# Attention times values, turned round: exponentials stationary, values and a column of ones moving, and a DMA transpose after it

## The chip, the cores and the metric

The kernel runs on one core of a Trainium2 chip. The metric is the device time of one execution in microseconds, the median of several; the profiled execution has a span of its own, about 2 us shorter. TensorE (PE in the profile) multiplies, VectorE (DVE) and ScalarE (ACT) work elementwise, GpSimd (POOL) helps, SyncE (SP) issues the DMAs.

## The reference, cut to what matters

Cosine attention over 8 batches, 12 heads, 448 positions and 64 channels, then a feed-forward part with 3584 tokens:

```python
scores = np.matmul(q_n, k_n.transpose(0, 1, 3, 2)) / tau      # q_n, k_n: rows scaled to length 1
attn = np.exp(scores - max); attn = attn / sum(attn)
x = (attn @ v)  ->  (3584, 768)
h = x @ w_in;  g = h * sigmoid(1.702 * h);  out = g @ w_out   # 768 -> 2048 -> 768
```

The kernel keeps the scores with keys on partitions and works on pairs of heads: 48 pairs, six to a batch.

## The kernel before

A planner written in Python walks all operations with estimated durations before the kernel is built and fixes the order on each engine. The first two batches (pairs 0 to 11) go through a half-width path with exponentials stationary, 112 columns at a time. The other 36 pairs have values stationary, one attention block for each head:

```python
def attend(x, j):                      # pair x, head j of the pair
    ps = ps_a.tile([128, S], FP32, tag="a")            # one bank, a single buffer
    for c in range(C):                                 # 4 chunks of 112 keys
        nc.tensor.matmul(out=ps,
            lhsT=vts[x % NV][:, c, j],                 # 112 x 128: 64 values, a one, zeros
            rhs=exps[x, c][:, j],                      # 112 x 448 exponentials move
            start=(c == 0), stop=(c == C - 1))
def attended(x, j):                    # VectorE: PSUM to SBUF, scaled, denominators as a row
    ...
# for each group of three pairs: two DMAs of the denominators to DRAM, one back as 112 x 24,
# a reciprocal on VectorE, one DMA out, two that spread it over 64 partitions each
def normalise(x):                      # VectorE: two multiplications SBUF x SBUF
    ...
```

The result stands with channels on partitions, as the feed-forward product wants it, but the denominators are one row that has to reach 64 partitions; hence the trip through DRAM.

## Time and profile before

| | before |
|---|---|
| median time | 471.35 us (3 runs), 470.99 with the run made beside the changed kernel |
| span of the profile | 467.7 us |
| busy TensorE / ScalarE / VectorE | 454.7 / 302.3 / 273.6 us |
| attention block, full width | 0.76 us, 72 of them |
| first score matmul of the full-width part | at 100.7 us |
| last attention block ends | at 402.9 us |

The lines behind it stand in the prediction. Idle time and distances given below without a line are taken from the starts and ends in the traces.

### The profile page before, as it was taken

The numbers are of one execution on the slowest core, as the hardware profiler recorded it, in microseconds if no ns is written. First come the engines' busy times: TensorE is split into PE (matmuls) and PEld (weight loads), VectorE is DVE, ScalarE is ACT, GpSimd is POOL, SyncE is SP. The second block draws the span as 40 slices with busy tenths as digits, with TensorE's granted clock in tenths as the row PEclk, the third lists the DMA queues.
The fourth block names the chain that finished last, engine by engine and source line by source line (L and its number), as shares of the span: only waits on it lengthen the run. The fifth ranks groups of instructions, "written<-read, shape, count | busy, mean of one in ns | idle before, by whom it ended". The sixth has DMA issues, their size and how long they took to land.

```text
span 467.7 us, 8829 instructions
## 1 busy us (share of the span) xinstructions
PE 454.7 (97%) x3306; PEld 259.6 (56%) x3306; DVE 273.6 (59%) x651; ACT 302.3 (65%) x478; POOL 146.7 (31%) x209
## 2 busy tenths in 40 slices
PE   8899999999999998999999999999999999999996
PEld 8778988644445544455445554455445554565563
DVE  6857986767899538682785539771463216523500
ACT  5878577879998567866886668755666457414421
POOL 2837573377354525133341505124010000000000
PEclk9999999999999999999999999999999999999999
DMA  8999098999976687455634747434301212021022
GB/s 234 245 241 244 4 196 185 265 253 310 251 163 160 142 189 167 119 142 150 170 96 111 214 126 166 132 97 103 84 2 31 69 35 64 1 78 54 1 68 69
DMA packets 81434, 63.49 MB, mean 136 GB/s; under 512 B 40232, under 2 KB 74864, under 8 KB 81392
## 3 DMA queue, kind: packets, MB, share of 16 engines
q1 hardware_dynamic: 77504, 56.41, 48.3%
q0 software_dynamic: 3648, 6.29, 7.4%
q8 instruction: 26, 0.43, 0.4%
q10 hardware_dynamic: 240, 0.23, 0.1%
q14 instruction: 16, 0.13, 0.1%
HBM read 49.81 MB, written 11.14 MB: 130 GB/s over the span
## 4 chain that ended last, share of the span: by engine, by line
PE 72%; DMA 10%; DVE 6%; ACT 4%; issue 3%; POOL 2%; SPq 2%; POOLq 0%; ACTq 0%; DVEq 0%
PE mm L575 25%; PE mm L520 23%; PE avp L384 9%; PE sp L365 6%; DMA w_out<-in_moe_w_out_dram 4%; PE tps L344 3%; PE mm L430 2%; POOL qks L316 2%; DMA q<-in_q_dram 2%; ACT expT L376 2%; DMA k<-in_k_dram 2%; DMA v<-in_v_dram 1%; PE mm L550 1%; DVE n L250 1%; PE sp L413 1%
## 5 line engine op out<-in xcount | busy, mean ns | idle before, releaser
L376 ACT ACTIVATE expT<-sp 112x896 f16<-112x896 f32 x192 | 166.7, 917 | 56.1 <-PE sp L365 44.8
L575 PE MATMUL mm<-w_out,gT 128*128 128x384 f16 x896 | 153.6, 326 | 0.7 <-DVE xT L463 0.7
L520 PE MATMUL mm<-xT,w_in 128*128 128x448 f16 x672 | 135.0, 353 | 1.9 <-DVE gT L537 1.9
L575 PEld LDWEIGHTS <-gT 128*128 128x128 f16 x896 | 84.3, 98 | 65.2 <-issue 12.7
L520 PEld LDWEIGHTS <-w_in 128*128 128x128 f16 x672 | 62.6, 98 | 68.7 <-issue 14.9
L537 DVE SCALAR_TENSOR_TENSOR gT<-th,mm 128x448 f16<-128x448 f16 x112 | 67.7, 617 | 54.5 <-ACT th L530 54.2
L530 ACT ACTIVATE th<-mm 128x448 f16<-128x448 f32 x128 | 69.4, 547 | 39.5 <-PE mm L520 31.4
L250 DVE TENSOR_REDUCE n<-sq 112x8 f32<-112x512 f32 x96 | 63.8, 677 | 33.4 <-ACT sq L244 32.0
L328 POOL CAST vt<-v 112x256 f16<-112x256 f32 x92 | 35.0, 400 | 130.9 <-PE avp L384 90.5
L401 DVE TENSOR_SCALAR av<-avp 65x448 f16<-65x448 f32 x72 | 44.5, 617 | 47.5 <-PE avp L384 47.2
L384 PE MATMUL avp<-expT,vt 112*128 112x448 f16 x288 | 66.4, 352 | 0.8 <-DVE av L401 0.8
L586 ACT ACTIVATE ost<-mm 128x384 f32<-128x384 f32 x56 | 27.4, 490 | 42.1 <-PE mm L575 40.5
L316 POOL TENSOR_TENSOR qks<-k,y 112x512 f16<-112x512 f32 x42 | 43.8, 1042 | 33.8 <-DVE y L291 26.4
L316 POOL TENSOR_TENSOR qks<-q,y 112x512 f16<-112x512 f32 x42 | 43.9, 1045 | 14.0 <-DVE y L291 8.0
L365 PE MATMUL sp<-qkT 64*112 64x448 f16 x288 | 42.9, 372 | 0.0
L384 PEld LDWEIGHTS <-vt 112*128 112x128 f16 x288 | 27.9, 97 | 25.9 <-issue 1.2
L508 DVE TENSOR_TENSOR xT<-av,rcb 64x448 f16<-64x448 f16 x72 | 31.0, 431 | 10.7 <-DMA rcb<-rcp 9.7
L244 ACT ACTIVATE sq<-k 112x512 f32<-112x512 f32 x42 | 26.5, 638 | 15.1 <-DMA k<-in_k_dram 12.6
L244 ACT ACTIVATE sq<-q 112x512 f32<-112x512 f32 x42 | 26.4, 633 | 6.0 <-DMA q<-in_q_dram 5.2
L365 PEld LDWEIGHTS <-qkT 64*112 64x112 f16 x288 | 13.3, 124 | 27.7 <-issue 26.5
L430 PE MATMUL mm<-vt,expT 112*112 112x65 f16 x384 | 23.9, 217 | 0.6 <-DVE xT L463 0.4
L430 PEld LDWEIGHTS <-expT 112*112 112x112 f16 x384 | 22.2, 132 | 2.2 <-issue 1.7
(47 smaller groups left out, 238.0 us busy)
## 6 DMA issues: line engine op xcount, KB each, us to landing
k<-in_k_dram SPq DMA_DIRECT2D x48, 224.0 KB, 2.9
v<-in_v_dram SPq DMA_DIRECT2D x48, 224.0 KB, 3.6
q<-in_q_dram SPq DMA_DIRECT2D x47, 224.0 KB, 4.6
rcb<-rcp SPq DMA_DIRECT2D x24, 168.0 KB, 3.4
w_in<-in_moe_w_in_dram POOLq DMA_DIRECT2D x2, 1536.0 KB, 16.2
w_out<-in_moe_w_out_dram POOLq DMA_DIRECT2D x2, 1536.0 KB, 14.4
out_dram<-ost SPq DMA_DIRECT2D x7, 336.0 KB
out_dram<-ost SPq DMA_DIRECT2D x8, 288.0 KB
```

The lines of the kernel that those rows point to most:

```text
L244: return nc.scalar.activation(out=sqs[x, ti], in_=src, func=AF.Square)
L250: nc.vector.tensor_reduce(out=n2s[grp][:, x - grp[0], ti], in_=sqs.pop((x, ti)), axis=AX.X, op=ALU.add,)
L316: return eng.tensor_tensor(out=qkss[x][:, ti].rearrange("p c j d -> p j c d"), in0=src, in1=rss[x][:, ti, :, :, None].to_broadcast((P, 2, ...
L365: nc.tensor.matmul(out=sp[:, j, :S], lhsT=qkT[64 * j : 64 * (j + 1), 1, c * P : (c + 1) * P], rhs=qkT[64 * j : 64 * (j + 1), 0, :], start= ...
L376: nc.scalar.activation(out=e, in_=sps.pop(key)[:, :, :S], func=AF.Exp, scale=inv_tau, **kw)
L384: nc.tensor.matmul(out=ps, lhsT=vts[x % NV][:, c, j], rhs=exps[x, c][:, j], start=(c == 0), stop=(c == C - 1),)
L401: nc.vector.tensor_scalar(out=avs[x][:n, j], in0=ps[:n], scalar1=AV_SCALE, scalar2=None, op0=ALU.mult)
L430: nc.tensor.matmul(out=ps[:P, o : o + D + 1], lhsT=exps[x, h, c // 2][:, j, at : at + P], rhs=vts[x % NV][:, c, j, 63 * j : 63 * j + D + 1 ...
L520: nc.tensor.matmul(out=ps[:, :S], lhsT=w_in_sb[:, kk, 128 * m : 128 * (m + 1)], rhs=xTs[b, kk], start=(kk == 0), stop=(kk == KT1 - 1),)
L530: nc.scalar.activation(out=ths[key], in_=mms[key][:, :S], func=AF.Tanh, scale=0.851)
L537: nc.vector.scalar_tensor_tensor(out=gts[b // 2][:, m, (b % 2) * S : (b % 2 + 1) * S], in0=ths.pop((b, m)), scalar=1.0, in1=mms.pop((b, m) ...
L575: nc.tensor.matmul(out=mms[b2, t, n][:, :NW], lhsT=gts[b2][:, kk, 128 * t : 128 * (t + 1)], rhs=w_out_sb[:, kk, NW * n : NW * (n + 1)], st ...
```

## The change

Its intent: let the 65 columns of values and ones move past 128 stationary exponentials. The output then has queries on partitions, the denominator is a column beside the values, and a reciprocal and one multiplication finish it. A DMA transpose brings it back to channels on partitions.

```diff
-    vts = [const.tile([P, C, 2, 128], FP16, ...) ...]
+    vts = [const.tile([P, C, 2, D + 1], FP16, ...) ...]   # head 0's values, ones, head 1's values
+    ets = [const.tile([P, 2 * S + 64], FP16, ...) ...]    # exponentials, 64 ones after them
 def attend(x, j):
-    for c in range(C):
-        nc.tensor.matmul(out=ps, lhsT=vts[...][:, c, j], rhs=exps[x, c][:, j], ...)
+    for t in range(4):
+        for c in range(C):
+            q0 = j * S + 128 * t
+            nc.tensor.matmul(out=ps[:, (D + 1) * t : (D + 1) * (t + 1)],
+                lhsT=exps[x, c][:, q0 : q0 + 128],
+                rhs=values(x, c, D * j, D * j + D + 1), ...)
-def attended / den_out / den_in / den_rcp / rcp_out / rcp_in / normalise   (cut)
+def normalise(x, j):
+    nc.vector.reciprocal(out=r, in_=ps[:, :, 0 if j else D])            # 128 x 4
+    nc.vector.tensor_tensor(out=xfs[x][:, :, j], in0=ps[:, :, j : j + D], in1=r..., op=ALU.mult)
+def turn(x):
+    nc.sync.dma_start_transpose(out=xTs[b, hp]..., in_=xfs.pop(x)...)   # 128 x 512
 # the planner's duration of a block
-    add(("at", x, j), "PE", 0.757, ...)
+    add(("at", x, j), "PE", 0.475, ...)
```

448 queries are three and a half tiles of 128. The fourth tile of a head reads 64 columns too many (the next head's, or the ones) and its spare rows are never used.

More of the change, by code (lines that the diff above doesn't have):

```diff
@@ L19 @@
 RS_A, RS_B = 0.703952253, 0.703952253 * 2.38924456
-AV_SCALE = 2.0**-11
 SEM_US = 0.1
@@ L174 @@
     GRP = 3
-    NV = 6
+    NV, NE = 6, 8
     NQK = 7
@@ L200 @@
     p_qkT = pool("p_qkT", 7)
-    p_exp = pool("p_exp", 8)
-    p_av = pool("p_av", 2)
     p_xs = pool("p_xs", 3)
+    p_xf = pool("p_xf", 3)
     p_rc = pool("p_rc", 2)
@@ L208 @@
     p_o = pool("p_o", 2)
-    dram = ctx.enter_context(tc.tile_pool(name="dramp", bufs=3, space=bass.MemoryType.DRAM))
     ps_s = psum("ps_s", 2)
@@ L219 @@
     w_out_sb = wpool.tile([128, KT2, DM], FP16, name="w_out")
-    vts = [const.tile([P, C, 2, 128], FP16, name=f"vt{i}") for i in range(NV)]
+    vts = [const.tile([P, C, 2, D + 1], FP16, name=f"vt{i}") for i in range(NV)]
+    ets = [const.tile([P, 2 * S + 64], FP16, name=f"et{i}") for i in range(NE)]
     if shift > 0:
@@ L321, in scale, with values @@
         )
+    def values(x, c, e0, e1):
+        return vts[x % NV][:, c].rearrange("p j e -> p (j e)")[:, e0:e1]
     def cast_v(x):
@@ L327, in cast_v @@
         return tuple(
-            copy(out=vt[:, :, j, 64 * j : 64 * j + D], in_=src[:, j]) for j in range(2)
+            copy(out=vt[:, :, j, :D], in_=src[:, j]) for j in range(2)
         )
@@ L356, in dma_transposed @@
         )
-    tpss, exps, avs, sps, avps, xss = [{} for _ in range(6)]
+    tpss, exps, sps, avps, xss = [{} for _ in range(5)]
     def scores(x, c):
@@ L373, in exp @@
     def exp(*key):
-        e = p_exp.tile([P, 2, S], FP16, name="expT")
+        e = exps[key] = ets[len(exps) % NE]
         kw = dict(bias=ebias[:P]) if shift > 0 else {}
         nc.scalar.activation(
-            out=e, in_=sps.pop(key)[:, :, :S], func=AF.Exp, scale=inv_tau, **kw
+            out=e[:, : 2 * S].rearrange("p (j s) -> p j s", j=2),
+            in_=sps.pop(key)[:, :, :S],
+            func=AF.Exp,
+            scale=inv_tau,
+            **kw,
         )
-        exps[key] = e
@@ L381, in attend @@
     def attend(x, j):
-        ps = ps_a.tile([128, S], FP32, name="avp", tag="a")
-        for c in range(C):
-            nc.tensor.matmul(
-                out=ps,
-                lhsT=vts[x % NV][:, c, j],
-                rhs=exps[x, c][:, j],
-                start=(c == 0),
-                stop=(c == C - 1),
-            )
-        avps[x, j] = ps
-    def attended(x, j):
-        if j == 0 and x % GRP == 0:
-            av = p_av.tile([128, GRP, 2, S], FP16, name="av")
-            for i in range(GRP):
-                avs[x + i] = av[:, i]
-            avgs[x // GRP] = av
-        n = D + 1 if j == 0 else 128
-        ps = avps.pop((x, j))
-        nc.vector.tensor_scalar(
-            out=avs[x][:n, j], in0=ps[:n], scalar1=AV_SCALE, scalar2=None, op0=ALU.mult
+        ps = avps[x, j] = ps_a.tile([128, 512], FP32, name="avp", tag="a")
@@ new lines, in attend @@
+        for t in range(4):
+            for c in range(C):
+                q0 = j * S + 128 * t
+                nc.tensor.matmul(
+                    out=ps[:, (D + 1) * t : (D + 1) * (t + 1)],
+                    lhsT=exps[x, c][:, q0 : q0 + 128],
+                    rhs=values(x, c, D * j, D * j + D + 1),
+                    start=(c == 0),
+                    stop=(c == C - 1),
+                )
+    def normalise(x, j):
+        ps = avps.pop((x, j))[:, : 4 * (D + 1)].rearrange("p (t e) -> p t e", t=4)
+        r = p_rc.tile([128, 4], FP32, name="rcx")
+        nc.vector.reciprocal(out=r, in_=ps[:, :, 0 if j else D])
+        if j == 0:
+            xfs[x] = p_xf.tile([128, 4, 2, D], FP16, name="xf")
+        nc.vector.tensor_tensor(
+            out=xfs[x][:, :, j],
+            in0=ps[:, :, j : j + D],
+            in1=r[:, :, None].to_broadcast((128, 4, D)),
+            op=ALU.mult,
+        )
@@ L403, in attended @@
+    def turn(x):
+        b, hp = x // HP, x % HP
+        xTs[b, hp] = p_x.tile([128, 512], FP16, name=f"xT{hp}")
+        nc.sync.dma_start_transpose(
+            out=xTs[b, hp].rearrange("p (t s) -> p t s", t=4),
+            in_=xfs.pop(x).rearrange("p t j d -> p (t j d)"),
         )
@@ L428, in attend_h @@
                 for c in range(C):
-                    at = (c % 2) * SH + i * P
+                    at = j * S + (c % 2) * SH + i * P
                     nc.tensor.matmul(
                         out=ps[:P, o : o + D + 1],
-                        lhsT=exps[x, h, c // 2][:, j, at : at + P],
-                        rhs=vts[x % NV][:, c, j, 63 * j : 63 * j + D + 1],
+                        lhsT=exps[x, h, c // 2][:, at : at + P],
+                        rhs=values(x, c, D * j, D * j + D + 1),
                         start=(c == 0),
@@ L461, in turned_h @@
         if h == 0:
-            xTs[b, hp] = p_x.tile([128, S], FP16, name=f"xT{hp}")
+            xTs[b, hp] = p_x.tile([128, 512], FP16, name=f"xT{hp}")
         (nc.scalar.copy if x in XA and not h else nc.vector.tensor_copy)(
@@ L466, in turned_h @@
         )
-    avgs, dens, dnms, rcps, rcbs, xTs = [{} for _ in range(6)]
-    def den_out(g, j):
-        if j == 0:
-            dens[g] = dram.tile([2, GRP, S], FP16, name="den")
-        row = D - j
-        nc.sync.dma_start(out=dens[g][j : j + 1], in_=avgs[g][row : row + 1, :, j])
-    def flat(t):
-        return t.rearrange("j i s -> (j i s)").rearrange("(p f) -> p f", p=P)
-    def den_in(g):
-        dnms[g] = p_rc.tile([P, 2 * GRP * S // P], FP16, name="dnm")
-        nc.sync.dma_start(out=dnms[g], in_=flat(dens.pop(g)))
-    def den_rcp(g):
-        r = p_rc.tile([P, 2 * GRP * S // P], FP16, name="rcg")
-        with nc.allow_low_precision("fp16 reciprocal of softmax denom"):
-            nc.vector.reciprocal(out=r, in_=dnms.pop(g))
-        dnms[g] = r
-    def rcp_out(g):
-        rcps[g] = dram.tile([2, GRP, S], FP16, name="rcp")
-        nc.sync.dma_start(out=flat(rcps[g]), in_=dnms.pop(g))
-    def rcp_in(g, j):
-        if j == 0:
-            rcbs[g] = p_rc.tile([128, GRP, S], FP16, name="rcb")
-        nc.sync.dma_start(
-            out=rcbs[g][64 * j : 64 * (j + 1)],
-            in_=rcps[g][j][None].to_broadcast((64, GRP, S)),
-        )
-    def normalise(x):
-        b, hp = x // HP, x % HP
-        xT = p_x.tile([128, S], FP16, name=f"xT{hp}")
-        av = avs.pop(x)
-        for j in range(2):
-            r = slice(64 * j, 64 * (j + 1))
-            last = nc.vector.tensor_tensor(
-                out=xT[r], in0=av[r, j], in1=rcbs[x // GRP][r, x % GRP], op=ALU.mult
-            )
-        xTs[b, hp] = xT
-        return last
+    xTs, xfs = {}, {}
     gts, mms, ths, osts = {}, {}, {}, {}
@@ L522, in mm1 @@
                 lhsT=w_in_sb[:, kk, 128 * m : 128 * (m + 1)],
-                rhs=xTs[b, kk],
+                rhs=xTs[b, kk][:, :S],
                 start=(kk == 0),
@@ L623 @@
     plan = Plan(
-        dict(q=NQK, k=NQK, v=4, sq=2, qks=6, vt=NV, qkT=7, sp=2, a=1, exp=8, av=6, xs=3)
+        dict(q=NQK, k=NQK, v=4, sq=2, qks=6, vt=NV, qkT=7, sp=2, a=1, exp=NE, xs=3, xf=3)
         | dict(x=2 * HP, mm=3, th=3, g=1, ost=2, port=1)
@@ L638 @@
     for x in range(NPAIR):
-        s, grp, g, first = due_of(x), group_of[x], x // GRP, x < HP
+        s, grp, first = due_of(x), group_of[x], x < HP
         early = due_of(grp[0]) - (4 if first else 8)
@@ L702 @@
             if j == 1:
-                es.append(("av", x, 0))
-            add(("at", x, j), "PE", 0.757, s + 2 + j, partial(attend, x, j), after=es,
+                es.append(("nx", x, 0))
+            add(("at", x, j), "PE", 0.475, s + 2 + j, partial(attend, x, j), after=es,
                 takes=[("a", 1)], frees=[("exp", 4 * j), ("vt", j)])
-            add(("av", x, j), "DVE", 0.54, s + 2 + j, partial(attended, x, j), after=[("at", x, j)],
-                takes=[("av", 1 - j)], frees=[("a", 1)])
-            if x % GRP == GRP - 1:
-                add(("den", g, j), "SP", 0.45, s + 2 + j, partial(den_out, g, j),
-                    after=[("av", y, j) for y in range(x - GRP + 1, x + 1)], dma=packets(GRP, 2 * S))
-        if x % GRP == GRP - 1:
-            ds = [("den", g, j) for j in range(2)]
-            add(("din", g), "SP", 0.45, s + 3, partial(den_in, g), after=ds, dma=packets(P, 48))
-            add(("rcp", g), "DVE", 0.25, s + 3, partial(den_rcp, g), after=[("din", g)])
-            add(("rout", g), "SP", 0.45, s + 3, partial(rcp_out, g), after=[("rcp", g)], dma=packets(P, 48))
-            for j in range(2):
-                add(("rin", g, j), "SP", 0.6, s + 3, partial(rcp_in, g, j), after=[("rout", g)],
-                    dma=packets(64, 2 * GRP * S))
-        rin = [("rin", g, 0), ("rin", g, 1)]
-        add(("x", x), "DVE", 0.75, 2 * (g + 1) * GRP + 3, partial(normalise, x), after=rin,
-            takes=[("x", 1), ("port", 1)], frees=[("av", 1), ("port", 1)])
+            add(("nx", x, j), "DVE", 0.55, s + 2 + j, partial(normalise, x, j), after=[("at", x, j)],
+                takes=[("xf", 1 - j)], frees=[("a", 1)])
+        add(("x", x), "SP", 1.0, s + 4, partial(turn, x), after=[("nx", x, 1)],
+            takes=[("x", 1)], frees=[("xf", 1)], dma=packets(256, 512))
     moe = []
@@ L806 @@
     for vt in vts:
-        nc.vector.memset(vt[:, :, 0, D:128], 0.0)
-        nc.vector.memset(vt[:, :, 1, 0:64], 0.0)
         nc.vector.memset(vt[:, :, 0, D : D + 1], 1.0)
-        nc.vector.memset(vt[:, :, 1, D - 1 : D], 1.0)
+    for et in ets:
+        nc.vector.memset(et[:, 2 * S :], 1.0)
     def link(late, first):
```

## The prediction

> **What bounds the kernel now.** I read the engine table first, then the chain of waits, then a table of engines by stage, then single matmul groups. The engine table says that TensorE (PE) is busy 97% of the span, but a matmul's recorded duration overlaps its neighbours', so this alone proves little. What proves it is the end of the chain, followed from 374 us on:
>
> ```profile
> 376.12 0.76 PE avp L384 x4
> 376.88 0.52 PE sp L365 x4
> 377.40 3.36 PE mm L575 x20
> 380.75 0.76 PE avp L384 x4
> 381.51 0.52 PE sp L365 x4
> ...
> 399.85 2.27 PE mm L520 x12
> 402.12 0.76 PE avp L384 x4
> 402.88 5.68 PE mm L520 x30
> 408.56 15.60 PE mm L575 x96
> 424.16 18.16 PE mm L520 x96
> 442.31 20.82 PE mm L575 x128
> ```
>
> Columns: start, length (us), engine, line, count. Each piece begins where the last one ended: PE is limited by issuing its matmuls. The pieces also give the true pace, which the group means (326 to 372 ns) hide: 18.16 us / 96 = 189 ns for 448 moving columns, 15.60 / 96 = 162.5 ns for 384. The attention block that the change rewrites (avp, line 384) is four matmuls of 448 columns, 0.76 us. There are 288 / 4 = 72 of them (36 pairs of heads, two heads each), none after 403 us. From 403 us to the end only the feed-forward products run, 65 us which the change can't touch.
>
> The stage table (busy time and count by engine; borders chosen at the first score matmul of the full-width attention, at the end of the crowded stretch of ScalarE, and at the last attention block):
>
> ```profile
> core 0: us, PE busy (x) PEld busy (x) DVE busy (x) ACT busy (x) POOL busy (x), PEclk, DMA share, GB/s
> 100.70:127.00 26.30, 26.30 (x147) 11.25 (x147) 18.78 (x44) 26.09 (x41) 16.60 (x25) 1.00 1.11 277
> 127.00:403.00 276.00, 273.36 (x1569) 135.25 (x1569) 163.35 (x354) 186.68 (x291) 74.48 (x106) 1.00 0.48 117
> 403.00:462.80 59.80, 59.80 (x350) 33.96 (x348) 16.46 (x30) 17.78 (x34) 0.00 (x0) 1.00 0.17 49
> ```
>
> In the middle stage, 276 us long, PE is full and ScalarE (ACT) is at 68%, VectorE (DVE) at 59%: PE alone sets the pace. In the stage before it, ACT is full as well (26.09 of 26.30 us): there two engines bind together, and relieving one gives nothing. This stage has 36 of the 288 attention matmuls, 9 blocks of the 72.
>
> **What the Trainium skill says, and whether the trace agrees.**
> "TensorE: Matmul & The Clock Gate", section "Back-to-back issue gap", gives an isolated gap of columns / 2.4 + 2.5 ns. The trace agrees: 189.2 and 162.5 ns for 448 and 384 columns. The same section's figure of about 81 ns for 128 columns in a stream with weight loads doesn't hold here: a run of 35 filler transposes of 128 columns takes 1.95 us in the chain, 56 ns each.
> The same page, section "Weight-path perf modes", says that a fast weight load is used when the number of weight columns is 128 and the type is not FP32, never for fewer. The trace shows its mark, in the weight-load rows of the full-width attention (128 columns, vt) and of the half-width attention of the first two batches (112 columns, expT):
>
> ```profile
> L384 PEld LDWEIGHTS <-vt 112*128 112x128 f16 x288 | 27.9, 97 | 25.9 <-issue 1.2 <-POOL qks L316 0.2
> L430 PEld LDWEIGHTS <-expT 112*112 112x112 f16 x384 | 22.2, 132 | 2.2 <-issue 1.7 <-ACT expT L376 0.2
> L430 PE MATMUL mm<-vt,expT 112*112 112x65 f16 x384 | 23.9, 217 | 0.6 <-DVE xT L463 0.4
> ```
>
> More columns load in less time, 97 against 132 ns. Line 430 is the decisive precedent: it already computes values with exponentials stationary and 65 columns moving, in the first two batches. Its blocks of 16 take 0.82 us in the chain when undisturbed, 51 to 52 ns a matmul. Streaming 65 columns would be 29.6 ns, and 112 weight columns at one per 2.4 GHz cycle are 46.7 ns: it is bound by its slow weight loads, and load and stream overlap, for their sum would be about 74 ns. The change takes 128 exponential columns (the last tile of a head reads 64 columns past it, and its spare rows are thrown away), which should buy the fast load.
> "SBUF — State Buffer", section "Who interferes with whom", says that a VectorE instruction with two SBUF inputs contends with a GpSimd one that reads SBUF, and one with at most one SBUF input outside the two-port modes doesn't. The trace agrees in part: the removed normalisation reads two SBUF tiles, its 72 instructions have median 389 ns, and one takes 1290.
>
> **The change, part by part.**
> Removed: 288 matmuls at 189 ns, 54.4 us of PE. 72 evictions at 617 ns, 72 multiplications at 431 ns and 12 reciprocals at 295 ns: 44.4 + 31.0 + 3.5 = 79 us of VectorE. Six DMAs per group of three pairs, 72 in all, for the trip of the denominators through DRAM (the large ones 24 of 168 KB). Some memsets at the start, hidden behind the first loads.
> Added on PE: 72 x 16 = 1152 matmuls of 65 columns with 128 weight columns. If the fast load hides, the pace is the stream's: 65 / 2.4 + 2.5 = 29.6 ns, an estimate from the skill's formula, which the trace bears out at larger sizes. 16 x 29.6 = 0.473 us a block (the change's own schedule books 0.475) against 0.756: 0.283 us saved per block, 20.4 us over 72. The block does 16 x 65 = 1040 moving columns for 4 x 448 = 1792; the gain is smaller in columns than a full 128-wide use would give because one tile in four is half empty.
> Added on VectorE: 72 reciprocals of 128x4 and 72 multiplications of 128x256 from PSUM. The half-width path has both, on 112 partitions: 176 and 424 ns. 72 x 0.600 = 43 us, so VectorE loses 36 us of work. It isn't the bound, so this counts only for stalls.
> Added on the DMA side: 36 transposes of 128x512. The 36 existing transposes (112x1024) take 1.25 us to issue and land in 4.1 us; the new ones move 57% as many bytes. They take the place of a chain of four dependent DMAs, so the input of the feed-forward arrives earlier, not later.
> Moved: comparing the instruction orders, the PE order is the same before full-width attention, nearly the same blockwise from about 127 us (block, four scores, 12 to 20 products) and the same in the tail. Changes between 64-row scores and full-row matmuls go from 220 to 224: nothing.
>
> The sum. In the stage 100.7 to 127 us the changed order holds nearly the same exponentials, tanh and squares, so ACT keeps its 26 us and the 9 blocks there give nothing: 9 x 0.283 = 2.5 us of the gain is lost as PE idle time. The other 63 blocks lie where PE alone binds: 63 x 0.283 = 17.8 us. In that stage the timeline shows three PE pauses, 0.77 us at 170 (waiting for an eviction), 1.41 at 178 and 0.46 at 294 (each for a gate on VectorE behind a burst of normalisations or norms), 2.6 us together. Less VectorE work and no bursts of six multiplications should save about half: 1.3 us. Against it I charge 1.0 us for new waits that I can't see. 471.35 - 17.8 - 1.3 + 1.0 = 453.3 us, 3.8% faster.
>
> **The rivals.**
> First, the weight load isn't hidden. If load and stream add up, using the 13 ns that the fast load would need at four times the column rate (an estimate), a block is 16 x 43 = 0.69 us: 63 x 0.07 = 4 us saved, 467 us. If 128 exponential columns load no faster than line 430's, 53 to 56 ns, a block is 0.87 us: 72 x 0.11 = 8 us lost, 479 us. For: no matmul of this trace with a full-row weight load runs below 48 ns, so a pair at 30 ns has no precedent. Against: the 97 ns loads, the overlap at line 430, and transposes with 128 weight columns and 112 moving at 49 ns, which is exactly their stream (112 / 2.4 + 2.5).
> Second, ScalarE becomes the bound. For: it already is for 26 us. Against: in the middle stage its 186.7 us would fill 72% of 258 us. If it bound locally after 127 us for a few cycles, I would lose another 2 to 3 us: 456.
> Third, the transposes queue behind loads and stores on the one SyncE queue, or delay the score transposes there. For: 72 transposes instead of 36 and an in-order queue. Against: six issues per group fall away, and the chain in the middle stage carries DMAs only around 140 to 170 us and at 283. If each of six batches waited 1 us: 459.
> Fourth, everything goes well and ACT's stage shortens too, because fewer VectorE waits let it run ahead: 450.
>
> **Range and chances.** The pace per matmul carries most of the doubt. I give 80% to 29 to 34 ns (450 to 457 us), 12% to 35 to 45 (457 to 467), 8% to more. Range 449.5 to 462. The limit of 2% is 461.9, so faster 0.86, within 2% 0.09, slower 0.05.
>
> **What would show it.** The values-times-queries weight loads should be near 98 ns, not 132, and blocks of 16 should take 0.47 us in the chain; 0.82 or more would sink the prediction. PE should show pauses of 2 to 3 us in total between 100 and 127 us with ACT still full, and hardly any after. VectorE's busy time should fall by about 35 us. The time from the last attention block to the end should stay at 65 us. If the gain is there but feed-forward blocks wait for xT, the third rival is real; if ACT is over 90% after 127 us, the second.

## The result, and the profile after

| | before | after |
|---|---|---|
| median time | 470.99 us (4 runs) | 454.03 us (4 runs, 451.52 to 454.85) |
| ratio, 95% interval | | 0.9637 (0.9587 to 0.9688) |
| span of the profile | 467.7 us | 452.9 us |
| busy VectorE | 273.6 us | 239.3 us |
| first score matmul of the full-width part | 100.7 us | 102.0 us |
| from there to the end of the last attention block | 302.1 us | 286.3 us |
| after it | 64.8 us | 64.6 us |

A ratio is the mean time of one kernel's fast runs over the mean of the other's in the same rounds, so it isn't quite the ratio of the medians.

The chain of waits of the changed kernel, late in its attention (start, length, engine, line, count; line 393 is the block):

```profile
359.76 0.48 PE avp L393 x16
360.24 0.52 PE sp L367 x4
360.76 2.71 PE mm L548 x16
363.46 0.49 PE avp L393 x16
...
388.31 5.68 PE mm L493 x30
393.98 15.60 PE mm L548 x96
409.58 18.16 PE mm L493 x96
```

The block fell from 0.76 to 0.48 us and everything round it kept its length; the tail starts at 388.31 instead of 402.88 us and its pieces are the same. From the groups of the page, the new weight loads, matmuls and VectorE instructions:

```profile
L393 PEld LDWEIGHTS <-et 112*128 112x128 f16 x1152 | 44.5, 97 | 15.9 <-PE sp L367 2.2
L393 PE MATMUL avp<-vt,et 112*128 112x65 f16 x1152 | 47.9, 193 | 2.9 <-DVE xf L407 1.6
L404 DVE RECIPROCAL rcx<-avp 128x4 f32<-128x4 f32 x72 | 12.8, 178 | 57.9 <-PE avp L393 57.9
L407 DVE TENSOR_TENSOR xf<-avp,rcx 128x256 f16<-128x256 f32 x72 | 30.5, 424 | 2.5
```

The loads have 97 ns, the mark of the fast kind. The 193 ns of the matmul is its recorded length, which overlaps that of its neighbours; the starts in the trace are 29 to 30 ns apart, with 33 to 35 at about every fourth one, so a block of 16 is 0.485 us. The stage table with the borders of the prediction's first stage and of the last block:

```profile
100.70:127.00 26.30, 25.31 (x245) 13.34 (x243) 18.58 (x45) 25.02 (x39) 17.90 (x27) 1.00 1.15 264
127.00:388.00 261.00, 258.86 (x2336) 150.05 (x2335) 133.81 (x348) 187.70 (x294) 74.06 (x106) 0.99 0.55 130
388.00:448.00 60.00, 60.00 (x359) 34.20 (x356) 14.18 (x24) 18.23 (x35) 0.00 (x0) 1.00 0.15 43
```

ScalarE is at 72% in the long stage (187.70 of 261), VectorE at 51%, TensorE full: the bound hasn't moved. One thing is new. The clock column is 0.99 there, and finer windows show where:

```profile
101.00:124.00 23.00, 22.67 (x205) 11.67 (x204) 15.86 (x38) 22.12 (x34) 16.80 (x25) 1.00 1.18 268
124.00:128.50 4.50, 2.87 (x55) 1.92 (x54) 3.85 (x12) 4.40 (x7) 0.81 (x2) 1.00 1.00 210
128.50:132.00 3.50, 3.50 (x19) 1.16 (x14) 2.40 (x9) 2.39 (x4) 1.83 (x2) 0.51 1.31 266
```

TensorE pauses at 125 and 127 us, busy 2.87 of 4.50 us while ScalarE has 4.40. By the trace these two pauses (0.65 and 0.97 us) wait for VectorE's multiplication, which frees the single bank. Then the granted clock is 0.51 for 3.4 us, by an estimate 1.7 us of work lost. The profile of the kernel before has no such stretch before its end. Nine of the fourteen profiles have one or two, each 3.4 or 6.8 us long, at places from 59 to 280 us; so a profile is best compared with another by stretches that both ran at full clock.

### The profile page after: what moved, and what is told of

Same layout as the page of the kernel before. It is cut to its first block, busy times and chain, and to the rows that moved or that the text cites. A ratio compares the mean times of both kernels' runs of the same rounds, so it can differ in the third digit from the quotient of the medians.

```text
span 452.9 us, 10559 instructions
## 1 busy us (share of the span) xinstructions
PE 439.0 (97%) x4170; PEld 276.6 (61%) x4170; DVE 239.3 (53%) x629; ACT 302.4 (67%) x478; POOL 146.3 (32%) x209
## 4 chain that ended last, share of the span: by engine, by line
PE 76%; DMA 11%; DVE 4%; ACT 3%; issue 2%; SPq 2%; POOL 1%; ACTq 0%; POOLq 0%; DVEq 0%
PE mm L493 28%; PE mm L548 25%; PE avp L393 7%; PE sp L367 7%; DMA w_out<-in_moe_w_out_dram 4%; DMA k<-in_k_dram 4%; PE tps L346 4%; PE mm L447 2%; DMA q<-in_q_dram 2%; DMA v<-in_v_dram 2%; ACT et L378 1%; PE mm L523 1%; PE sp L430 1%; ACT sq L242 1%; POOL qks L314 1%
## 5 line engine op out<-in xcount | busy, mean ns | idle before, releaser
L378 ACT ACTIVATE et<-sp 112x896 f16<-112x896 f32 x192 | 166.6, 916 | 37.1 <-PE sp L367 25.9
L548 PEld LDWEIGHTS <-gT 128*128 128x128 f16 x896 | 84.3, 98 | 64.6 <-issue 12.0
L393 PEld LDWEIGHTS <-et 112*128 112x128 f16 x1152 | 44.5, 97 | 15.9 <-PE sp L367 2.2
L393 PE MATMUL avp<-vt,et 112*128 112x65 f16 x1152 | 47.9, 193 | 2.9 <-DVE xf L407 1.6
L404 DVE RECIPROCAL rcx<-avp 128x4 f32<-128x4 f32 x72 | 12.8, 178 | 57.9 <-PE avp L393 57.9
L407 DVE TENSOR_TENSOR xf<-avp,rcx 128x256 f16<-128x256 f32 x72 | 30.5, 424 | 2.5
L447 PE MATMUL mm<-vt,et 112*112 112x65 f16 x384 | 23.9, 217 | 1.4 <-DVE xT L480 1.0
L447 PEld LDWEIGHTS <-et 112*112 112x112 f16 x384 | 22.1, 132 | 3.2 <-issue 2.2
L346 PE MATMUL tps<-ident 128*128 128x128 f16 x250 | 18.1, 234 | 3.3 <-DVE qkT L350 2.0
## 6 DMA issues: line engine op xcount, KB each, us to landing
w_in<-in_moe_w_in_dram POOLq DMA_DIRECT2D x2, 1536.0 KB, 16.9
```

The costliest lines, as they stand in the source:

```text
L346: nc.tensor.transpose(out=tps0[:, 2 * S : 2 * S + 128], in_=ident, identity=ident)
L378: nc.scalar.activation(out=e[:, : 2 * S].rearrange("p (j s) -> p j s", j=2), in_=sps.pop(key)[:, :, :S], func=AF.Exp, scale=inv_tau, **kw,)
L393: nc.tensor.matmul(out=ps[:, (D + 1) * t : (D + 1) * (t + 1)], lhsT=exps[x, c][:, q0 : q0 + 128], rhs=values(x, c, D * j, D * j + D + 1), ...
L447: nc.tensor.matmul(out=ps[:P, o : o + D + 1], lhsT=exps[x, h, c // 2][:, at : at + P], rhs=values(x, c, D * j, D * j + D + 1), start=(c == 0),
L548: nc.tensor.matmul(out=mms[b2, t, n][:, :NW], lhsT=gts[b2][:, kk, 128 * t : 128 * (t + 1)], rhs=w_out_sb[:, kk, NW * n : NW * (n + 1)], st ...
```

## The experiments

Twelve kernels ran. All results were correct but for the one that is wrong on purpose. The run with 112 columns and the three paddings were made on one chip; the repeat, the squares, the transfer times and the first batches on a second; the other four on a third; each beside the kernel before; so ratios are compared, not times. The changed kernel itself was run again in the second series:

> The changed kernel itself once more, as the yardstick for the others of this series on the same chip. Expected 0.964 of the kernel before, 452 to 455 us.

Measured: 0.9662 (0.9627 to 0.9697), 453.69 us. This is the yardstick below. Its profile has the pauses at 125 and 127 us but no half-speed stretch before the end: the first score matmul to the start of the thirteenth attention block (twelve blocks, 108 products and 56 scores, "the crowded stage" from here on) took 37.8 us, where the profile of the changed kernel above took 39.8. From there to the last matmul of the last block ("the late stage") every kernel has the same 1026 products, 232 scores and 60 blocks: 263.15 us before, 246.26 in the changed kernel, 246.23 here.

### Is it the fast weight load?

```diff
-                q0 = j * S + 128 * t
+                q0 = j * S + 112 * t        # four tiles of 112: 448 exactly
-                    lhsT=exps[x, c][:, q0 : q0 + 128],
+                    lhsT=exps[x, c][:, q0 : q0 + 112],
   # (cut: 112 rows in place of 128 in normalise and turn)
```

> The changed kernel with tiles of 112 queries in place of 128 in the full-width attention: as many matmuls of 65 moving columns, same orders, but no weight load has 128 columns. Theory (the fast weight load makes the pace): weight loads near 132 ns in place of 97, 51 to 52 ns from matmul to matmul in place of 29, a block of 16 takes 0.83 us in place of 0.485, and the time grows by up to 72 x 0.345 = 25 us, less about 3 us where ScalarE is full: 475 to 479 us, slower than the kernel before. Rival (the stream of 65 columns makes the pace whatever the load): 453 to 455 us.

Measured: 1.0113 (1.007 to 1.0156), 475.18 us. The groups:

```profile
L393 PEld LDWEIGHTS <-et 112*112 112x112 f16 x1152 | 70.9, 132 | 11.4 <-PE sp L367 1.5 <-ACT et L378 0.8 <-issue 0.6
L393 PE MATMUL avp<-vt,et 112*112 112x65 f16 x1152 | 70.7, 216 | 1.5 <-DVE xf L407 0.9 <-ACT et L378 0.7
```

and its chain, two pieces:

```profile
386.41 0.81 PE avp L393 x16
387.22 0.52 PE sp L367 x4
```

As many matmuls with as many moving columns, fewer rows out, less data for the transpose, and yet 0.81 us a block where 0.485 was. Sixteen columns fewer turn a gain of 3.5% into a loss of 1.1%. The padding to 128 isn't tidiness: without it the whole change loses.

### Is the gain TensorE time alone?

```diff
+        for n in (252, 252, 130):              # after each block, into unused columns of its bank
+            nc.tensor.matmul(out=ps[:, 260 : 260 + n], lhsT=exps[x, 0][:, :128],
+                rhs=exps[x, 1][:, :n], start=True, stop=True)
```

> The changed kernel with three useless matmuls (252, 252 and 130 moving columns, 0.27 us by their streams) after each attention block, into spare columns of its bank, so that a block is as long on TensorE as in the kernel before; all that the change took from VectorE and the DMAs stays taken. Theory (TensorE time alone is the gain): 62 or 63 blocks x 0.27 = 17 us back, 470 to 472 us, the same as before. Rival (the lighter VectorE and the four dropped DMA hops carry part of the gain): 467 us or less.

Measured: 0.999 (0.9954 to 1.0026), 469.53 us against 469.35. The chain shows the padding as intended, 0.49 + 0.27 = 0.76 us:

```profile
371.43 0.49 PE avp L393 x16
371.92 0.27 PE avp L402 x3
372.19 0.52 PE sp L367 x4
```

So the order, the lighter VectorE and the four DMA hops that fell away bring nothing together, within the 1.7 us of the interval. By stages of the profile this is a balance, though: the crowded stage took 40.5 us against 38.6 in the kernel before, the late stage 260.2 against 263.15, with none of the 2.6 us of pauses that the kernel before has there. Which of the three took the pauses away isn't separated.

### Where is TensorE's time worth something?

The same padding in ten blocks only, in two places:

```diff
-        for n in (252, 252, 130): ...
+        if 40 <= x < 45: for n in (252, 252, 130): ...     # or: if x < 17
```

> The same padding in ten attention blocks of the late stage (pairs 40 to 44), where TensorE alone was found to bind. Theory: 10 x 0.27 = 2.7 us more than the changed kernel, 456.5 to 457 us, and in the profile the stretch from the first score matmul to the last attention block 2.7 us longer. Rival (there is slack there as well): no change, 454 us.

Measured: 0.9731 (0.9696 to 0.9767). In the profile, the stretch from the first padded block to the block after the last takes 44.48 us against 41.76 in the changed kernel: 2.72 us more, all that was added; every other profile with blocks of the new length has 41.76 there too, the kernel before 44.49. TensorE alone binds there. In the ratio it is 0.7% above the yardstick, 3 us. The stretch that the expectation named, from the first score matmul to the last block, grew by 4.2 us against the yardstick and not by 2.7: pauses inside blocks at 167 and 268 us, before the padded ones, came on top.

> The same padding in the first ten attention blocks alone (pairs 12 to 16), which lie where ScalarE is full. Theory (those blocks gained nothing, so they lose nothing when lengthened again): 453 to 455 us, at most 1 us more than the changed kernel; if the padding also keeps TensorE awake, the half-speed stretch of 3.4 us near 130 us of the changed kernel goes and the time falls by up to 1.7 us. Rival (TensorE binds there too): 2.7 us more, 456.5 us or above.

Measured: 0.9712 (0.9677 to 0.9747), 0.5% above the yardstick, which is inconclusive by itself. By the profile the expectation failed: from the first score matmul to the eleventh block 32.4 us against 29.9 in the yardstick, 2.5 of the 2.7 us added. (No half-speed stretch lies near 130 us in this profile, as hoped, but one of 3.4 us at 280, so the total settles nothing.) So these blocks had gained nearly nothing by being shortened (the crowded stage took 38.6 us before and 37.8 in the yardstick, 0.8 gained of 12 x 0.27), and still aren't free to be lengthened. The stage tables over the crowded stage, of the kernel before,

```profile
100.74:139.38 38.64, 38.64 (x214) 16.90 (x214) 30.02 (x67) 38.01 (x60) 24.03 (x35) 1.00 1.00 240
```

of the yardstick,

```profile
102.43:140.25 37.82, 36.13 (x357) 19.54 (x357) 28.47 (x72) 37.20 (x58) 23.93 (x35) 1.00 1.15 248
```

and with the early padding

```profile
102.34:142.62 40.28, 39.03 (x388) 21.18 (x388) 28.54 (x72) 37.82 (x58) 24.05 (x35) 1.00 1.06 234
```

show ScalarE (the fourth engine) at 98% in the first two and 94% in the third. In the padded one neither engine is full; by the trace the exponentials wait 1.2 us for scores, and TensorE 1.1 us for VectorE's multiplication, which frees the single bank, and 0.2 for exponentials. With before's lengths in the new order (the padding everywhere) this stage took 40.5 us against 38.6 in the old order: at the old lengths the new order, which here has three blocks in a row without a product between them, is the worse one. That asked for the next run.

### Order or engine?

```diff
-    add(("at", x, j), "PE", 0.475, ...)
+    add(("at", x, j), "PE", 0.757, ...)        # plan as before, run as changed
```

> The changed kernel planned with the old length of an attention block (0.757 us in place of 0.475), so that instructions stand in the order of the kernel before, which alternates block, scores and product in the crowded stage and never has three blocks in a row; the instructions themselves are the changed ones. Theory (ScalarE's own work, some 37 us to the twelfth block, bounds that stage in any order): from the first score matmul to the twelfth block 37 to 38.5 us, as in the kernel before (38.6) and in the changed kernel undisturbed (37.8), total within 1 us of it, ratio 0.962 to 0.967. Rival (the new order's blocks in a row and their single bank cost the gain): 36 us or less to the twelfth block, pauses of TensorE there under 1 us, 1 to 2 us less in all, ratio 0.960 to 0.962.

Measured: 0.9713 (0.9685 to 0.9741). The crowded stage, with the same work in it:

```profile
101.05:139.06 38.01, 36.90 (x358) 20.36 (x357) 28.61 (x74) 37.57 (x60) 24.23 (x36) 1.00 1.13 252
```

38.0 us, ScalarE 99% busy: with faster blocks in the old order the stage is as long as in the new, which speaks for ScalarE's work as its floor. The rival of the order fell for this stage. The total was outside what either expected, 0.5% above the yardstick, with intervals that overlap; in the profile it is the late stage that is longer, 248.4 us against 246.2.

### Can ScalarE be relieved there?

```diff
-    SQP = range(HP, 2 * HP)                      # pairs whose squares GpSimd takes
+    SQP = (*range(HP, 2 * HP), 21, 22, 23)
```

> The changed kernel with the squares of pairs 21 to 23 (six instructions of some 0.53 us on ScalarE) moved to GpSimd, where the crowded stage of ScalarE has room. Theory (ScalarE being full near 100 to 130 us costs the change its gain there, and the pauses it makes let the TensorE clock fall to half for 3.4 us): no three attention blocks in a row without a product between, no half-speed stretch there, 2 to 4 us less than the changed kernel, ratio to the kernel before 0.956 to 0.960. Rival (those pauses have another cause, the single accumulator bank waiting for VectorE): no change, 0.964.

Measured: 0.9648 (0.9618 to 0.9679), the same as the yardstick within its interval, a miss. The crowded stage did what the theory said:

```profile
99.54:136.09 36.55, 35.74 (x358) 19.29 (x358) 27.88 (x71) 33.55 (x51) 30.05 (x42) 1.00 0.84 206
```

ScalarE down to 33.55 us, TensorE the fuller of the two, 1.3 us less than the yardstick, and no three blocks stand in a row any more. (There is no half-speed stretch, but the yardstick has none either, so that half of the theory wasn't tested.) But new pauses of 0.6 to 0.7 us came at 145, 146, 173 and 179 us, and counted from the first score matmul the 21st block started 72.3 us later, 72.2 in the yardstick. Something later took the gain; three of these pauses wait for exponentials, and ScalarE waits 25.2 us in all for the loads that feed its squares.

### Late loads behind an in-order engine

In the list of waits (who waited for whom, us in all, times, longest), the kernel before has

```profile
ACT sq L244 <- DMA k<-in_k_dram: 12.6, 10, 2.6
```

and the changed one

```profile
ACT sq L242 <- DMA k<-in_k_dram: 22.8, 18, 3.1
```

(The yardstick has 19.0.) A square that waits for its load holds up the exponentials queued behind it on ScalarE; the attention block, now shorter, comes to its third matmul before the third exponential chunk is there. In the timeline of the changed kernel ScalarE stands for 2.80 us before a square, takes the exponentials only then, and a block breaks in two:

```profile
265.57 0.63 ACT L242 ACTIVATE sq<-k 112x512 f32<-112x512 f32 x1 [2.80 <-DMA k<-in_k_dram]
267.71 0.26 PE L393 MATMUL avp<-vt,et 112*128 112x65 f16 x3
268.25 0.57 PE L393 MATMUL avp<-vt,et 112*128 112x65 f16 x13 [0.28 <-ACT et L378]
```

The planner books 1.9 us for any DMA on top of the transfer time that it works out itself (0.85 us for a k load that has the engines alone). The page of the changed kernel has a median of 4.5 us from issue to landing of the k loads, and the new transposes hold SyncE for 1.21 us each where 1.0 is booked. The edit books the measured issue and a longer, not a measured, time for every DMA:

```diff
-DMA_US = 1.9
+DMA_US = 2.9
-        add(("x", x), "SP", 1.0, ...)
+        add(("x", x), "SP", 1.21, ...)
```

> The changed kernel with its planner told the truth about transfers: 2.9 us in place of 1.9 from issue to landing, and 1.21 in place of 1.0 us to issue the new transpose. Nothing else changes than the order of instructions: squares are queued on ScalarE later against their loads. Theory (squares that wait for late loads hold back the exponentials behind them on the in-order ScalarE, and attention blocks of the faster TensorE then pause after their second matmul): ScalarE's waits for the q and k loads fall from 29 us in all to under 15, the pauses inside attention blocks after 140 us go from 2 us to under 0.5, 1 to 3 us less than the changed kernel. Rival (these waits are hidden): within 1 us of it.

Measured: 0.9592 (0.9561 to 0.9622), 0.7% below the yardstick. The wait fell as the theory asked:

```profile
ACT sq L242 <- DMA k<-in_k_dram: 4.2, 4, 2.6
```

and with q's 4.2 us it is 8.4 in all (23.2 in the yardstick). No attention block of this profile after 140 us has a pause. The new order also moves the first score matmul to 96.5 us and 36 products from before it into the crowded stage (43.7 us), but these two cancel: the thirteenth block starts at 140.19 us, 140.25 in the yardstick. The gain lies in the late stage, 243.89 us against 246.23: 2.3 us, as the theory asked.

### The same trick where TensorE isn't alone

```diff
-        at = j * S + (c % 2) * SH + i * P           # half-width path, batches 0 and 1
-                        lhsT=exps[x, h, c // 2][:, at : at + P],
+        at = j * S + (c % 2) * SH + i * 128
+                        lhsT=exps[x, h, c // 2][:, at : at + 128],
   # outputs, reciprocals, transposes to 128 rows; planner: 0.48 us a block
```

> The change taken to the first two batches as well: their half-width attention uses 128 exponential columns in place of 112, so that its weight loads are of the fast kind; transposes and copies follow. Blocks there should go from 0.82 to 0.48 us, 24 x 0.34 = 8 us less TensorE work. Theory (TensorE isn't what binds in the first 100 us; loads and ScalarE are): 0 to 3 us less than the changed kernel. Rival (TensorE binds there too): 7 to 8 us less, 446 us.

Measured: 0.9581 (0.9545 to 0.9617), 0.8% or 3.8 us below the yardstick, between the two expectations. The loads went to 97 ns, and a block in the chain to 0.58 us or so with the first start's wait in it:

```profile
39.00 0.59 PE mm L447 x16
54.67 0.58 PE mm L447 x16
```

From the distances of starts, TensorE's attention there lost about 8 us, and 2.1 us of it went straight into 38 more of the filler matmuls that the planner puts into TensorE's idle time at the start. Less than half of the saving reached the total, but more reached the end of the first stage: the first score matmul of the full-width part came at 95.9 us, where runs with the yardstick's order have 101.0 to 103.8, and the thirteenth block at 135.19 against 140.25. So TensorE binds in more of the first 100 us than the total shows. Part was lost later: this profile has a half-speed stretch of 3.4 us at 125 us, and its late stage took 247.96 us against 246.23, with pauses.

### Together

> The two edits that won, together: the planner with true transfer times, and 128 exponential columns in the first two batches too. If their gains add (0.7% and 0.8% against the changed kernel's repeat): ratio to the kernel before 0.951, 447 us. If both only shorten the same first 100 us: 0.957.

Measured: 0.9592 (0.9572 to 0.9612). The gains don't add. Its late stage is that of the longer transfer times, 243.89 us, so this gain is there whole; what is missing is the first batches' lead, for the thirteenth block starts at 139.38 us and not near 135. Its profile has TensorE idle for 2.9 us from 56 and for 1.9 from 88, and half-speed clock after the second. The first pause stands in the profile of the longer transfer times alone too; the second, as long, in neither.

> The same with the six squares on GpSimd as well. These gave 0.15% by themselves, within the noise; expected the same as the pair of edits, 0.949 to 0.957.

Measured: 0.957 (0.9546 to 0.9593), 449.25 us median. Its interval lies below the yardstick's, so it beats both kernels, by 1% and 4.3%; it isn't told apart from the 128-column half-width path alone (0.9581) or the planner's alone (0.9592).

### What sets the 29 ns?

```diff
+                n = D + 1 if c == 0 else 33          # wrong result on purpose
-                    rhs=values(x, c, D * j, D * j + D + 1),
+                    rhs=values(x, c, D * j, D * j + n),
```

> A wrong result on purpose, one look: in the full-width attention three of four matmuls of a block move 33 columns in place of 65, with the same 128-column weight loads. What sets the 29 ns between matmuls? If the stream: 33 / 2.4 + 2.5 = 16 ns for the short ones. If an issue floor as the skill gives it, about 25 ns. If the weight load: 29 ns still, and a block of 0.456 us from first to last start as before.

Measured in one look: wrong result, as meant, 451.75 us. Starts after a 33-column matmul are 25 ns apart, and a block in its chain is

```profile
345.00 0.41 PE avp L394 x16
345.41 0.52 PE sp L367 x4
```

0.41 us. Starts after a matmul of 65 columns are still 29 to 30 ns apart in this run, so the number of moving columns sets the pace at 65. At 33 it is 25 and not 16: something else holds it there, and one size in one look doesn't tell an issue floor from the weight load. Half the columns gain only 4 ns a matmul.

## Why the prediction was right

The median came at 454.03 us against 453.3 predicted. By its steps:

**TensorE alone sets the pace.** Shown for the late stage: 2.72 us added there cost 2.72, and of the 16.9 us that it lost, 16.3 are 60 blocks. With the old length put back everywhere the ratio is 0.999, but as a balance of a longer crowded and a shorter late stage.

**The pace of 29.6 ns by a fast load that hides.** Shown, by 29 to 30 ns in the trace and by the 112-column kernel. The block is 0.485 us instead of 0.473, for the starts of 33 to 35 ns; the saving is 0.271 us a block, 0.9 us less over all 72 than the 20.4 predicted. The first rival, load and stream adding up, is out. One figure on the way is not shown: the 46.7 ns for a load of 112 columns assumes a column per cycle, which no run measures; the runs have 51 to 52 ns for load and stream in a row.

**The blocks of the crowded stage give nothing.** Nearly right in size: twelve blocks gave 0.8 of 3.3 us in the undisturbed repeat. The reason given, that ScalarE is full, is shown by the old order running into the same 38 us with ScalarE at 99%, and by the stage shrinking when squares left ScalarE. In the new order the shorter blocks did gain there (40.5 us with the padding, 37.8 without), but that order itself had cost 1.9. What the prediction didn't see is that in the new order TensorE stays just as tight, so time put back there costs too, and that the clock can be halved after pauses there (in one of the two profiles of this kernel).

**The other blocks give 17.8 us.** The late stage went from 263.2 to 246.3 us, 16.9 us for 60 blocks, of which 60 x 0.271 = 16.3 is the blocks.

**Pauses: 1.3 us saved, 1.0 charged.** The net was right, the parts were too small, and that they nearly cancel is luck. With the padding everywhere the late stage has no pause, so all 2.6 us were saved; the shorter blocks brought back 2.4 (246.3 us against the 243.89 of the three kernels without pauses). The gate pauses at 178 and 294 us went. Others came: 0.85 us inside the block at 167 us, and 0.2 to 0.5 inside four blocks between 250 and 277. These are the second and third rival in small: not the transposes' results come late (no product waits for them; they land in 2.5 us), but loads on their queue, through ScalarE. The transposes alone don't do it: with the padding everywhere they are all there and the k loads take a median of 4.1 us (2.9 before), yet ScalarE waits 16.0 us for q and k loads, 17.8 before and 29.0 in the changed kernel. It takes the shorter blocks as well. That booking longer times takes the waits away is shown.

**The rest.** VectorE lost 34 us of work (predicted 35), the tail stayed, ScalarE came to 72% in the long stage (predicted 72%). The start of the full-width part at 102.0 us instead of 100.7 stays open: the order up to there is the same, but the eight profiles that share it began between 101.0 and 103.8, all later than the one of the kernel before. The two-input multiplications that the change removed did meet GpSimd: the 64 that ran while it was idle took 376 to 391 ns, the 8 that overlapped its work 412 to 1290. All 72 new ones, which read one operand from PSUM, took 423 to 427, 41 of them beside GpSimd's work.

## What to carry to other kernels

When a matmul has a thin operand, let the thin one move and keep the stationary side at exactly 128 columns, with padding if need be: here 128 gave 29 ns a matmul and 112 gave 52, the difference between a gain and a loss. Take the pace from the distances of matmuls that follow each other and price only the stages where the engine binds alone; the stage with two full engines gave 0.8 of 3.3 us here. After speeding up one engine, look at what the engines beside it wait for, and check the planner's transfer times against the profile: longer ones gave 2.3 us here.

## What the Trainium skill lacked or had wrong

- "TensorE: Matmul & The Clock Gate", section "Back-to-back issue gap": its sustained 81 ns for 128 columns with weight loads doesn't hold here; 128 columns go at 56 ns, 65 at 29 to 30 with a fast load for each. Its floor of about 25 ns agrees with the 33-column run, with a weight load for every matmul.
- The same page, section "LDWEIGHTS (loading the stationary operand)": columns / 1.2 ns would be 93 ns for 112 columns; a load and a matmul of 65 together take 52 ns in a stream. The section on weight-path modes doesn't say what the fast load buys a thin fp16 matmul: 52 to 29 ns, recorded load 132 to 97.
- The same page, section "What's actually happening", has the clock fall to half after an idle window of 3.4 us. Here it was at 0.51 for 3.4 us after a stretch in which TensorE was busy 2.87 of 4.50 us, and in the yardstick's profile the same pauses, busy 2.87 of 4.50 us again, had no such effect. The page gives no figure for how little activity is enough to lose the clock, and these runs give none.
- "DMA: Bandwidth & Descriptors", section "DMA Transpose (X-bar)", has no figure for how long one transpose between SBUF tiles holds the issuing engine on this chip: 128x512 of fp16 held SyncE for 1.21 us and landed in 2.5 (medians of 36).
